# Joining sign, exponent and middle bits in two VectorE steps, in the weight split that opens a convolution and maxout kernel

## The chip, the cores and the metric

The kernel runs on one core of a Trainium2 chip. The metric is the device time of one launch in microseconds, the median of several runs. A core has five engines that run at once: TensorE (PE in the profile, with its weight loads as PEld), VectorE (DVE), ScalarE (ACT), GpSimd (POOL) and SyncE (SP, which here only issues DMA). Each executes its own queue strictly in order and waits on semaphores of the others.

## The reference

```
w   = softmax(weight_gen, over the 7 taps)            # weight_gen: 8 x 4160 x 8 heads x 7
out[s, head] = sum_k w[s, head, k] * x[s - 6 + k, head]   # x: 8 x 4160 x 192, zeros ahead of s = 0
t   = out as 33280 tokens x 192
h   = max(t @ w1, t @ w2, t @ w3)                     # w1, w2, w3: 192 x 768
y   = h @ w_out                                       # w_out: 768 x 192
```

The matrices w1, w2, w3 and w_out arrive as float64. A 64-bit word is read here as two 32-bit words: the high one holds the sign, 11 bits of exponent and the top 20 bits of the mantissa.

## The kernel before

The tokens are cut into 65 chunks of 512 (four columns t of 128 tokens). For each chunk: GpSimd multiplies x with the softmax weights (`product`, L246, tile r; tokens x0.0 to x0.3 in the list below are the four of chunk 0), VectorE sums the seven taps (`total`, L261, tokens +0.0 to +0.3), the result is transposed (`transpose`, tokens t; on TensorE for the first three chunks), and `parts` (tokens p) splits it into a high part (xa_hi, by ScalarE) and a low part (xa_lo, xb: by VectorE for the first three chunks, by GpSimd later). The softmax runs once for three chunks (tokens s0, s1, ...): VectorE red (L215), GpSimd subtract (L217), ScalarE Exp (L222), VectorE den, add, reciprocal (L224 to L226), GpSimd multiply (L229).

TensorE then runs nine `up` steps (k0 to k8: three pairs of column blocks times w1, w2, w3) of 18 matmuls each with 64 rows, the two halves of the rows side by side; a result is copied to m by ScalarE (L376, for w1) or merged into m by VectorE (L378, for w2 and w3). After w3, ScalarE makes h_hi (L381) and GpSimd h_lo (L385). `down` for chunk c-1 (96 matmuls) stands between k5 and k6 of chunk c, and its result is added by ScalarE and VectorE (L410, L411).

The weights must be ready in two parts, hi and lo, before the steps that use them. There are 18 units: a0 to a8 (128x256 each, upper 128 rows of w1 to w3), b0 to b2 (128x384, lower 64 rows of two blocks), d0 to d5 (128x192, w_out). Each goes through the generator `split` (L453 to L498), which issues its instructions in stages; a `yield` ends a stage. Before, one unit takes on VectorE five instructions: clamp (L481), shift and mask (L483), sign joined (L488), then the low bits (L494) and the exponent (L495) for the low part; on ScalarE four: absolute value (L470), a copy of the 32 middle bits to f (L476), hi (L493), f scaled (L497); on GpSimd the product lo = f * e (L498). All PSUM tiles of the kernel (`ps`, eight banks in turn) are shared by the splits, the transposes and the matmuls.

The order of work in the opening is the hand-written list `OPENING`: for each tick a row of names, and each name issues the next stage of that piece of work (or of what it needs first, through `finish`). A tick is half an `up` step; 22 ticks make a chunk, chunk 0 has no `down`. Tick -1 is all that stands ahead of the first matmul; what is not issued when a step needs it is finished there: `finish(p0)`, `finish(a_k)`, `finish(b_k/3)` ahead of step k of chunk 0, `finish(p1)` ahead of chunk 1 and all d ahead of `down` of chunk 0. From then on fixed places per chunk (`PRODUCTS`, `SUMS`, ...) hold. SP issues the loads at the start in the order super 0 of x, a-weights, b-weights, a-weights, super 1, a-weights, w_out.

Of the kernel before, what the change touches and what calls it, by code (L numbers as in the profile page):

```python
# [17 lines left out]
AF = mybir.ActivationFunctionType
ALU = mybir.AluOpType
AX = mybir.AxisListType  # L20

P = 128

OPENING = {
    -1: (
        "x0.0 x0.1 a0 a0 a1 a0 a1 x0.3 a2 a0 x0.2 a2 +0.0 a2 b0 b0 s1 +0.1 a1 a2 b0 +0.3 s1 "
        "a1 b0 s0 b1 +0.2 s1 a3 a3 a6"  # L30
# [3 lines left out]
    2: "s0",
    3: "a3 x1.0 b1 a6 b2 a5",
    4: "a4 a5 t0",
    5: "a4 x1.1",
    6: "t0",
    7: "s0",
    8: "+1.1 t0 b0 p0 t1 a4 s1 b1",  # L40
    9: "x1.3 a5 a7 b2",
    10: "s0 b2 +1.3",
    11: "+1.2",
    14: "p0 p0 b2",
    16: "a7 a8 p1",
    17: "a7 a8",
    18: "a7 s2 p1 d1",
    19: "d1 t1 a8 p1 b2 d2",
    20: "d2",
    21: "d1 b1 d0",  # L50
    22: "d0",
    24: "t1 +2.0",
    25: "d0 +2.1 d2",
    27: "d5 a8 d1 t1 d0",
    28: "d2 d3 d4",
    29: "d3",
    30: "d4",
    31: "d3 x2.2 d5 d4",
    32: "d5 +2.2 t2 x2.1 t2 x2.3",
    34: "t2 d4 +2.3",  # L60
    35: "x3.0 p2",
    36: "d3",
    37: "x2.0 x3.1 p2 p2",
    40: "+3.0",
    42: "s2",
    43: "t3",
    45: "d5 t3",
    46: "+3.3",
    47: "+3.2",
    49: "x4.1 t3 s2",  # L70
    52: "t3",
    54: "t3",
    55: "p3 x4.0",
    58: "t2",
    63: "+4.1",
    64: "p3",
    66: "s2 t3 x4.2",
    67: "x4.3 +3.1 t3",
    76: "+4.0 x3.3",
    78: "p3",  # L80
    85: "+4.3 +4.2",
    86: "x3.2",
# [8 lines left out]
LOAD = (5, 5)  # L93

ON_TENSOR = 3


@with_exitstack
def lightconv_maxout_kernel(
# [151 lines left out]

    def transpose(c):


        acc = state["acc", c]
        if c < ON_TENSOR:  # L270
            pa, pb = (ps.tile([P, CH], F32, name="ph") for _ in range(2))
            pb = pb[:DB]
            state["p", c] = pa, pb
            for t in range(TC):
                to = slice(t * P, (t + 1) * P)
                pin(nc.tensor.transpose(pa[:, to], acc[:, t, :P], ident))
                pin(nc.tensor.transpose(pb[:, to], acc[:, t, P:], ident))
                yield
            return
        v = xtp.tile([P, NJ * D * 2], F32, name="room", bufs=1)  # L280
        pa, pb = v[:, :CH], v[DB:, CH : 2 * CH]
        state["p", c] = pa, pb
        blocks = v[:, 2 * CH : 2 * CH + TC * D].rearrange("p (t d) -> p t d", t=TC)
        pin(nc.vector.transpose(blocks, acc))  # L284
        yield
        for f in range(0, D, 32):
            to = pa[f : f + 32] if f < P else pb[f - P : f - P + 32]
            to = to.rearrange("f (t p) -> f t p", t=TC)
            for p in range(0, P, 32):
                pin(nc.scalar.copy(to[:, :, p : p + 32], blocks[p : p + 32, :, f : f + 32]))  # L290
            yield

    def parts(c):
# [14 lines left out]
        pin(nc.scalar.copy(xb[:DB], xc[:DB].bitcast(F32)))  # L308
        pin(eng.tensor_tensor(xb[DB:], pb, xc[at].bitcast(F32), op=ALU.subtract))
        state["xT", c] = xa_hi, xa_lo, xb, xc  # L310

# [106 lines left out]
    begun = collections.deque()
    SETTLE = 2.8
# [21 lines left out]
            settle = SETTLE if f is down and args[0] < NC - 1 else 0.0  # L447
            begun.append((clock[0] + settle, f(*args, 1)))


    words = [w.bitcast(U32) for w in (w1, w2, w3, w_out)]

    def split(raw, hi, lo):  # L453

        high = raw[..., 1]


        n = int(np.prod(raw.shape[1:-1]))
        if 2 * n <= CH:
            both = ps.tile([P, CH], F32, name="ph")  # L460
            u, l = both[:, :n], both[:, n : 2 * n]
        else:
            u, l = (ps.tile([P, CH], F32, name="ph")[:, :n] for _ in range(2))
        e, f = (prep.tile([P, NU], F32, name=name, bufs=3)[:, :n] for name in ("e", "f"))
        f_words = f
        if len(raw.shape) == 4:
            u, l, e, f = (v.rearrange("p (i n) -> p i n", n=P) for v in (u, l, e, f))
        ui, li, ei = (v.bitcast(U32) for v in (u, l, e))

        pin(nc.scalar.activation(u, high.bitcast(F32), AF.Abs))  # L470
        yield
# [3 lines left out]
        pin(
            nc.scalar.copy(  # L476
                f_words.bitcast(U16).rearrange("p (n h) -> p n h", h=2),
                flat.bitcast(U16)[..., 1:3],
            )
        )  # L480
        pin(nc.vector.tensor_scalar(u, u, F_MAX, F_MIN, op0=ALU.min, op1=ALU.max))  # L481
        pin(
            nc.vector.tensor_scalar(  # L483
                ui, ui, 3, 0x3FFFF000, op0=ALU.logical_shift_left, op1=ALU.bitwise_and
            )
        )
        pin(
            nc.vector.scalar_tensor_tensor(  # L488
                ui, high, 0xC0000000, ui, op0=ALU.bitwise_and, op1=ALU.bitwise_or
            )  # L490
        )
# [3 lines left out]
        pin(nc.vector.tensor_scalar(ei, ui, 0xFF800000, None, op0=ALU.bitwise_and))  # L495
        yield
        pin(nc.scalar.activation(f, li, AF.Copy, scale=2.0**-36))  # L497
        pin(nc.gpsimd.tensor_tensor(lo, f, e, op=ALU.mult))  # L498
# [206 lines left out]
```

## Time and profile before

| | |
|---|---|
| median of 3 runs | 1698.19 us (1697.55 to 1698.21) |
| the profiled execution | 1699.39 us, span of its instructions 1697.6 us |
| busy over the span | PE 1657.2, PEld 1466.1, DVE 1124.6, ACT 1145.8, POOL 1426.2 us |
| granted TensorE clock, mean | 0.998 |
| HBM traffic | 51.25 MB read, 25.56 MB written, 45 GB/s over the span |

The page lists engines by busy time, the span in 40 slices, the chain of work that ended last, and groups of instructions by line with count, busy time, mean duration and the idle time ahead of them. The group rows name the tile written, then the tiles read, and the shape with partitions first. "Windows" are the same busy times for stretches of the span, "waits" name who was waited for, and the timeline lists instructions in order (neighbours of one kind merged, with their count).

### The profile page before, as it was taken

What the parts mean: (1) busy time and instruction counts of PE and PEld (TensorE: products, weight loads), DVE (VectorE), ACT (ScalarE), POOL (GpSimd) and SP (SyncE); (2) the same over time, 40 slices, a digit from 0 to 9 for tenths busy, and PEclk for the clock granted to TensorE, in tenths of its full rate; (3) what the DMA queues carried; (4) which work ended last, traced back from release to release, by engine and by line L of the source; (5) the groups of instructions that cost most, each with busy time, mean ns of one, the idle gap of its engine ahead of it and who ended that gap; (6) DMA issues with size and microseconds to landing.
All of it is one profiled execution on the core that took longest, in us unless ns stands there. A gap on an engine that the chain in (4) does not pass through costs nothing.

```text
span 1697.6 us, 42191 instructions
## 1 busy us (share of the span) xinstructions
PE 1657.2 (98%) x16794; PEld 1466.1 (86%) x16794; DVE 1124.6 (66%) x1552; ACT 1145.8 (67%) x2896; POOL 1426.2 (84%) x844
## 2 busy tenths in 40 slices
PE   3899999999999999999999999999999999999999
PEld 2598889889889889889988988988988988988998
DVE  7966766666666666666666666666666666666653
ACT  5657667667666766766766766766776776676672
POOL 6888888989888888888888888988888888888872
PEclk9999999999999999999999999999999999999999
DMA  7010101101010110101010110101011010101000
GB/s 236 1 70 10 70 29 52 70 20 60 20 70 15 66 70 21 60 21 70 11 70 21 60 70 20 61 20 70 11 70 61 27 63 20 70 11 46 20 11 29
DMA packets 20422, 79.51 MB, mean 47 GB/s; under 512 B 2320, under 2 KB 5128, under 8 KB 17536
## 3 DMA queue, kind: packets, MB, share of 16 engines
q1 hardware_dynamic: 20104, 76.54, 11.9%
q8 instruction: 131, 2.15, 0.5%
q14 instruction: 67, 0.55, 0.1%
q10 hardware_dynamic: 120, 0.28, 0.0%
HBM read 51.25 MB, written 25.56 MB: 45 GB/s over the span
## 4 chain that ended last, share of the span: by engine, by line
PE 94%; DVE 3%; ACT 1%; DMA 1%; POOL 1%; SPq 0%; issue 0%; DVEq 0%
PE ph L329 94%; DVE acc L261 1%; DVE m L378 0%; DMA wt<-in_weight_gen_dram 0%; DVE ph L483 0%; POOL r L246 0%; DVE ph L488 0%; DVE e L495 0%; DVE ph L481 0%; DVE ph L494 0%; DMA xt<-in_x_dram 0%; SPq L529 0%; ACT room L290 0%; SPq L521 0%; POOL h_lo L385 0%
## 5 line engine op out<-in xcount | busy, mean ns | idle before, releaser
L246 POOL TENSOR_TENSOR r<-xt,wt 128x1344 f32<-128x1344 f32 x260 | 721.4, 2814 | 0.6 <-DMA xt<-in_x_dram 0.4
L378 DVE TENSOR_TENSOR m<-ph,m 128x512 f32<-128x512 f32 x780 | 520.6, 685 | 197.4 <-PE ph L329 113.7
L329 PE MATMUL ph<-xa_hi,wa_hi 64*128 64x512 f32 x2340 | 630.8, 391 | 9.4 <-DVE m L378 3.1
L385 POOL TENSOR_TENSOR h_lo<-m,h_hi 128x512 fp32r<-128x512 f32 x390 | 503.3, 1301 | 161.7 <-ACT h_hi L381 157.0
L329 PE MATMUL ph<-xa_lo,wa_hi 64*128 64x512 f32 x2340 | 626.9, 388 | 1.0 <-DVE xa_lo L304 1.0
L329 PE MATMUL ph<-xa_hi,wa_lo 64*128 64x512 f32 x2340 | 626.1, 387 | 1.1 <-POOL wa_lo L498 1.1
L329 PE MATMUL ph<-xb,wb_hi 64*128 64x512 f32 x2340 | 626.0, 387 | 0.0
L329 PE MATMUL ph<-wo,h_hi 64*128 64x384 f32 x3120 | 595.5, 355 | 0.0
L329 PE MATMUL ph<-wo,h_lo 64*128 64x192 f32 x3120 | 522.3, 247 | 0.0
L381 ACT CAST h_hi<-m 128x512 fp32r<-128x512 f32 x390 | 241.8, 621 | 409.7 <-DVE m L378 406.6
L261 DVE TENSOR_REDUCE acc<-r 128x192 f32<-128x1344 f32 x260 | 401.8, 1547 | 125.5 <-POOL r L246 125.5
L290 ACT COPY room<-room 32x128 f32<-32x128 f32 x1488 | 440.8, 296 | 25.7 <-DVE room L284 7.5
L329 PE MATMUL ph<-xc,wb_lo 64*128 64x512 f32 x1170 | 453.1, 387 | 0.1
L329 PEld LDWEIGHTS ph<-wo,h_lo 64*128 64x128 f32 x3120 | 398.8, 188 | 2.5
L329 PEld LDWEIGHTS ph<-wo,h_hi 64*128 64x128 f32 x3120 | 398.4, 184 | 2.9 <-issue 0.4
L329 PEld LDWEIGHTS ph<-xa_hi,wa_hi 64*128 64x128 f32 x2340 | 338.7, 185 | 53.9 <-DVE m L378 3.9
L329 PEld LDWEIGHTS ph<-xa_hi,wa_lo 64*128 64x128 f32 x2340 | 338.4, 185 | 42.0 <-POOL wa_lo L498 1.5
L329 PEld LDWEIGHTS ph<-xa_lo,wa_hi 64*128 64x128 f32 x2340 | 338.7, 185 | 38.7 <-DVE xa_lo L304 1.5
L329 PEld LDWEIGHTS ph<-xb,wb_hi 64*128 64x128 f32 x2340 | 338.7, 185 | 38.4 <-ACT xb L308 0.3
L376 ACT COPY m<-ph 128x512 f32<-128x512 f32 x390 | 221.8, 586 | 38.5 <-PE ph L329 35.3
L411 DVE TENSOR_TENSOR o<-ph,ob 128x192 f32<-128x192 f32 x260 | 86.7, 353 | 234.5 <-ACT ob L410 234.5
L329 PEld LDWEIGHTS ph<-xc,wb_lo 64*128 64x128 f32 x1170 | 216.3, 185 | 20.9 <-POOL wb_lo L498 0.5
(54 smaller groups left out, 702.6 us busy)
## 6 DMA issues: line engine op xcount, KB each, us to landing
xt<-in_x_dram SPq DMA_DIRECT2D x20, 1728.0 KB, 7.1
out_dram<-o SPq DMA_DIRECT2D x64, 384.0 KB, 2.3
wt<-in_weight_gen_dram SPq DMA_DIRECT2D x21, 336.0 KB, 3.0
h_hi<-in_moe_w_dram SPq DMA_DIRECT2D x6, 256.0 KB, 4.8
xt<-in_x_dram SPq DMA_DIRECT2D x1, 1536.0 KB, 9.3
h_lo<-in_moe_w_dram SPq DMA_DIRECT2D x6, 192.0 KB, 4.8
room<-in_moe_w_out_dram SPq DMA_DIRECT2D x1, 1152.0 KB, 8.1
xt<-in_x_dram SPq DMA_DIRECT2D x1, 960.0 KB, 5.2
```

The source lines that it names most:

```text
L246: nc.gpsimd.tensor_tensor(r.rearrange("p (h g) k -> p k h g", g=G), xt[:, la + t : la + t + K].rearrange("p k (h g) -> p k h g", g=G), wt[ ...
L261: nc.vector.tensor_reduce(state["acc", c][:, t], r, axis=AX.X, op=ALU.add)
L290: pin(nc.scalar.copy(to[:, :, p : p + 32], blocks[p : p + 32, :, f : f + 32]))
L329: ins = nc.tensor.matmul(ph[:, :n], w[h], v[h], start=begins and half == 0 and q == 0, stop=ends and half == 1 and q == len(terms) - 1,)
L376: pin(nc.scalar.copy(m[:, :N], ph[:, :N]))
L378: pin(nc.vector.tensor_tensor(m[:, :N], ph[:, :N], m[:, :N], op=ALU.max))
L381: later(1, lambda: pin(nc.scalar.copy(hi, m[:, :N])))
L385: nc.gpsimd.tensor_tensor(lo, m[:, :N], hi.bitcast(F32), op=ALU.subtract)
L411: pin(nc.vector.tensor_tensor(o[:, t], po[:, :D], ob, op=ALU.add))
```

## The change

Three things change. First, the split. The absolute value u and the middle bits (`low`) are made as before, in one stage. Then the exponent is clamped and shifted to its place by two ScalarE Relus on the upper 16 bits of each word (or, for the nine units in `CLAMP_ON_POOL`, a GpSimd minimum and one Relu); the result goes to the upper halves of `tops`, three tiles that are set to 1 once at the start. VectorE joins in two instructions: `(low >> 13) | tops` to the PSUM tile v, and `(high & sign) | v`. ScalarE makes hi, and lo is now w - hi: on GpSimd for the eight units in `LO_ON_POOL` (for them w is in SBUF), on VectorE from PSUM for the other ten. A unit now has seven stages (a b unit one more, for its four copies to wb_hi). Second, six small GpSimd memsets at the start (`top`, `over`, `span`, `below`). Third, `OPENING` is rewritten. `BY_DMA` is empty, so no copy moves to a DMA queue.

```diff
 OPENING = {
     -1: (
-        "x0.0 x0.1 a0 a0 a1 a0 a1 x0.3 a2 a0 x0.2 a2 +0.0 a2 b0 b0 s1 +0.1 a1 a2 b0 +0.3 s1 "
-        "a1 b0 s0 b1 +0.2 s1 a3 a3 a6"
+        "x0.3 a0 a0 a0 s0 a1 x0.0 a0 a0 a2 x0.1 a1 a0 a1 +0.3 a1 a2 a0 a2 a1 a1 a2 +0.0 b0 a2 "
+        "x0.2 b0 a3 a2 a2 b0 a1 a3 b1 +0.1 b1 +0.2 b0 a3 b0 b1 b0 s1 b0 a3 b1 a3 b0 s1 a4 a5 "
+        "a4 b1 a6 s1 t0 a5 a6 x1.0 a3 a3 x1.2"
     ),
-    0: "a6 a3",
-    1: "a6 b1 a5 t0 +1.0 a4 x1.2",
...
+    1: "a6 a5 a6 a4 a5 b2 a6 b1 a5 p0 a5 s0 a4 x1.1 a7 a6 a4 s1 +1.0 a7 t0 t0",
+    3: "a4 +1.2",
+    8: "b2 a5 b1 b2 a8 x1.3 b2",
+    9: "b2 a7 t0 s0 d1 +1.3 +1.1 b2 a4 a8 t1 b1 a6",
+    16: "a8 a7 b2 b2 a7 a7",
+    17: "d1 x2.2 a8 d1 d0 p0 s2 d0 s0 t1 a7",
...
+    28: "d3",
+    31: "d3 d4",
+    32: "d5 t2 t2 +2.2 d4 d3 d3 x2.1 x2.0",
+    34: "d5",
+    35: "d2 d4 +2.3",
+    36: "p2 t2 x3.0 s2 p2 p2 +3.1",
...
 }
+LO_ON_POOL = ("a2", "a5", "a6", "b0", "d0", "d2", "d3", "d5")
+CLAMP_ON_POOL = ("a4", "a7", "a8", "b2", "d0", "d1", "d2", "d3", "d5")
+BY_DMA = ()
...
+    E_MIN = (1023 - 127) << 4
+    E_MAX = (255 << 4) - 1
     NU = 3 * P
+    top = [const.tile([P, NU], U32, name=f"top{k}") for k in range(3)]
+    turn = itertools.count()
+    over = const.tile([P, 1], F32, name="over")
+    span = const.tile([P, 1], F32, name="span")
+    below = const.tile([P, 1], F32, name="below")
+    F_MAX = float(np.array((E_MIN + E_MAX) << 16 | 0xFFFF, np.uint32).view(np.float32))
...
+    def split(raw, hi, lo, name):
...
+            u, v = both[:, :n], both[:, n : 2 * n]
+            u, v = (ps.tile([P, CH], F32, name="ph")[:, :n] for _ in range(2))
+        if name in CLAMP_ON_POOL:
+            u = prep.tile([P, NU], F32, name="u", bufs=2)[:, :n]
+        tops = top[next(turn) % len(top)][:, :n]
+        low = prep.tile([P, NU], U32, name="low", bufs=3)[:, :n]
         flat = raw.rearrange("p i n w -> p (i n) w") if len(raw.shape) == 4 else raw
+        pin(nc.scalar.activation(u, flat[..., 1].bitcast(F32), AF.Abs))
         pin(
             nc.scalar.copy(
+                low.bitcast(U16).rearrange("p (n h) -> p n h", h=2),
                 flat.bitcast(U16)[..., 1:3],
             )
         )
-        pin(nc.vector.tensor_scalar(u, u, F_MAX, F_MIN, op0=ALU.min, op1=ALU.max))
...
+        yield
+        upper = u.bitcast(U16).rearrange("p (n h) -> p n h", h=2)[..., 1]
+        to = tops.bitcast(U16).rearrange("p (n h) -> p n h", h=2)[..., 1]
+        if name in CLAMP_ON_POOL:
+            pin(nc.gpsimd.tensor_scalar(u, u, F_MAX, None, op0=ALU.min))
+            yield
+            pin(nc.scalar.activation(to, upper, AF.Relu, bias=below, scale=8.0))
+        else:
+            pin(nc.scalar.activation(u, upper, AF.Relu, bias=over, scale=-1.0))
+            yield
+            pin(nc.scalar.activation(to, u, AF.Relu, bias=span, scale=-8.0))
+        yield
+        w = prep.tile([P, NU], F32, name="w", bufs=2)[:, :n] if name in LO_ON_POOL else v
         pin(
             nc.vector.scalar_tensor_tensor(
+                v.bitcast(U32), low, 13, tops, op0=ALU.logical_shift_right, op1=ALU.bitwise_or
             )
         )
         yield
+        pin(
+            nc.vector.scalar_tensor_tensor(
+                w.bitcast(U32),
+                flat[..., 1],
+                0x80000000,
+                v.bitcast(U32),
+                op0=ALU.bitwise_and,
+                op1=ALU.bitwise_or,
+            )
+        )
+        yield
+        if len(raw.shape) == 4:
+            w = w.rearrange("p (i n) -> p i n", n=P)
+        pin(nc.scalar.copy(hi, w))
+        yield
+        eng = nc.gpsimd if name in LO_ON_POOL else nc.vector
+        pin(eng.tensor_tensor(lo, w, hi.bitcast(F32), op=ALU.subtract))
...
+    for t in top:
+        nc.gpsimd.memset(t, 1)
+    nc.gpsimd.memset(over, float(E_MIN + E_MAX))
+    nc.gpsimd.memset(span, float(8 * E_MAX))
+    nc.gpsimd.memset(below, float(-8 * E_MIN))
```

In the prediction, "first join" and "second join" are the two VectorE instructions of the new split; the first reads two tiles in SBUF (`low` and `tops`), the second one in SBUF and one in PSUM.

More of the change, by code (lines that the diff above doesn't have):

```diff
@@ L28 @@
     -1: (
-        "x0.0 x0.1 a0 a0 a1 a0 a1 x0.3 a2 a0 x0.2 a2 +0.0 a2 b0 b0 s1 +0.1 a1 a2 b0 +0.3 s1 "
-        "a1 b0 s0 b1 +0.2 s1 a3 a3 a6"
-    ),
-    0: "a6 a3",
-    1: "a6 b1 a5 t0 +1.0 a4 x1.2",
[L34 to L82, printed above, removed]
[3 rows of a table added]
+    ),
+    1: "a6 a5 a6 a4 a5 b2 a6 b1 a5 p0 a5 s0 a4 x1.1 a7 a6 a4 s1 +1.0 a7 t0 t0",
[4 more added lines that the diff above has]
+    17: "d1 x2.2 a8 d1 d0 p0 s2 d0 s0 t1 a7",
+    18: "d1 d2 p1",
+    19: "d1 t1 a8 p0",
+    20: "d1 d2 d0 d1 d0 d0",
+    21: "p1 d2 d2",
+    24: "d5 d4 a8 d0 t1 +2.0",
+    25: "d5 p1 d4 d3 d2 d5 +2.1",
+    27: "d2 d3 d3 d0 x2.3 s2 d4",
+    28: "d3",
[4 more added lines that the diff above has]
+    36: "p2 t2 x3.0 s2 p2 p2 +3.1",
+    42: "t3",
+    43: "t3 t3 d5 x3.3 x4.1 x4.2 x3.2 +3.2 a8 d5",
+    51: "x4.0",
+    55: "t3 t3 p3 x3.1 +4.1 +4.0 t3 d4 +4.2 x4.3",
+    58: "p3 +3.3",
+    59: "+4.3 +3.0",
+    60: "t2",
+    87: "t3",
+    90: "s2 p3",
 }
@@ L169, in lightconv_maxout_kernel @@
     wo = const.tile([P, NJ, 2 * D], F32R, name="wo")
-    F_MAX = float(np.array(0x47EFFFFF, np.uint32).view(np.float32))
-    F_MIN = float(np.array(0x38000000, np.uint32).view(np.float32))
+    E_MIN = (1023 - 127) << 4
+    E_MAX = (255 << 4) - 1
     NU = 3 * P
+    top = [const.tile([P, NU], U32, name=f"top{k}") for k in range(3)]
[4 more added lines that the diff above has]
+    F_MAX = float(np.array((E_MIN + E_MAX) << 16 | 0xFFFF, np.uint32).view(np.float32))
     halves = (slice(0, DB), slice(DB, P))
@@ L451, in lightconv_maxout_kernel @@
     words = [w.bitcast(U32) for w in (w1, w2, w3, w_out)]
-    def split(raw, hi, lo):
-        high = raw[..., 1]
+    def split(raw, hi, lo, name):
         n = int(np.prod(raw.shape[1:-1]))
@@ L460, in split @@
             both = ps.tile([P, CH], F32, name="ph")
-            u, l = both[:, :n], both[:, n : 2 * n]
+            u, v = both[:, :n], both[:, n : 2 * n]
         else:
[L463 to L471, printed above, removed]
+            u, v = (ps.tile([P, CH], F32, name="ph")[:, :n] for _ in range(2))
[3 more added lines that the diff above has]
+        low = prep.tile([P, NU], U32, name="low", bufs=3)[:, :n]
         flat = raw.rearrange("p i n w -> p (i n) w") if len(raw.shape) == 4 else raw
+        pin(nc.scalar.activation(u, flat[..., 1].bitcast(F32), AF.Abs))
         pin(
             nc.scalar.copy(
-                f_words.bitcast(U16).rearrange("p (n h) -> p n h", h=2),
+                low.bitcast(U16).rearrange("p (n h) -> p n h", h=2),
                 flat.bitcast(U16)[..., 1:3],
@@ L480, in split @@
         )
[L481 to L486, printed above, removed]
+        yield
[11 more added lines that the diff above has]
+        w = prep.tile([P, NU], F32, name="w", bufs=2)[:, :n] if name in LO_ON_POOL else v
         pin(
             nc.vector.scalar_tensor_tensor(
-                ui, high, 0xC0000000, ui, op0=ALU.bitwise_and, op1=ALU.bitwise_or
+                v.bitcast(U32), low, 13, tops, op0=ALU.logical_shift_right, op1=ALU.bitwise_or
             )
@@ L492, in split @@
         yield
-        pin(nc.scalar.copy(hi, u))
-        pin(nc.vector.tensor_scalar(li, f.bitcast(U32), 0x01FFFFFE, None, op0=ALU.bitwise_and))
-        pin(nc.vector.tensor_scalar(ei, ui, 0xFF800000, None, op0=ALU.bitwise_and))
-        yield
-        pin(nc.scalar.activation(f, li, AF.Copy, scale=2.0**-36))
-        pin(nc.gpsimd.tensor_tensor(lo, f, e, op=ALU.mult))
+        pin(
[8 more added lines that the diff above has]
+        )
+        yield
+        if len(raw.shape) == 4:
[4 more added lines that the diff above has]
+        pin(eng.tensor_tensor(lo, w, hi.bitcast(F32), op=ALU.subtract))
     room = [
@@ L544, in prepare_a @@
         pair = slice(2 * jp, 2 * jp + 2)
-        yield from split(raw, wa_hi[:, pair, i], wa_lo[:, pair, i])
+        yield from split(raw, wa_hi[:, pair, i], wa_lo[:, pair, i], f"a{u}")
     def prepare_b(jp):
@@ L549, in prepare_b @@
         hi = prep.tile([P, 3, P], F32R, name="hi", bufs=1)
-        yield from split(raw, hi, wb_lo[:, jp])
+        yield from split(raw, hi, wb_lo[:, jp], f"b{jp}")
+        yield
         for odd, h in enumerate(halves):
             for to in halves:
-                pin(nc.scalar.copy(wb_hi[to, 2 * jp + odd], hi[h].bitcast(F32)))
+                if f"b{jp}" in BY_DMA:
+                    pin(nc.sync.dma_start(out=wb_hi[to, 2 * jp + odd], in_=hi[h]))
+                else:
+                    pin(nc.scalar.copy(wb_hi[to, 2 * jp + odd], hi[h].bitcast(F32)))
     def prepare_down(j):
-        yield from split(raw_down[:, j], wo[:, j, :D], wo[:, j, D:])
+        yield from split(raw_down[:, j], wo[:, j, :D], wo[:, j, D:], f"d{j}")
+    for t in top:
[3 more added lines that the diff above has]
+    nc.gpsimd.memset(below, float(-8 * E_MIN))
     state["now"] = -1
```

## The prediction

> **What bounds the kernel now.** I read the windows first. Columns: stretch in us, its length, busy time and count on PE, PEld, DVE, ACT, POOL, granted clock, DMA share, GB/s.
>
> ```profile
> 9.00:30.00 21.00, 2.71 (x9) 1.21 (x9) 19.19 (x34) 12.59 (x29) 15.50 (x11) 1.00 0.90 284
> 30.00:63.00 33.00, 26.08 (x161) 16.84 (x163) 31.57 (x61) 26.20 (x58) 23.63 (x18) 1.00 0.19 74
> 63.00:82.00 19.00, 16.49 (x120) 11.51 (x118) 18.25 (x36) 9.28 (x25) 18.82 (x15) 0.91 0.00 1
> 95.00:1650.00 1555.00, 1554.80 (x15913) 1384.06 (x15911) 1029.47 (x1379) 1074.29 (x2739) 1339.49 (x779) 1.00 0.12 44
> ```
>
> From 95 us on TensorE is idle for 0.2 us in 1555, so nothing of a change in the opening is lost or won there, as long as GpSimd (86% busy) keeps up: what shifts the opening shifts the end, one for one. In the opening it is VectorE that never rests: 69.0 of the 73 us from 9 to 82. TensorE at its later rate (15913 matmuls in 1555 us, 10.2 per us) would need 28 us for the 290 recorded there. The chain of waits says the same: it runs along VectorE until 77 us, then leaves for TensorE for good, but for one visit to GpSimd.
>
> ```profile
> 76.41 0.37 DVE ph L488
> 77.67 3.90 PE ph L329 x18
> 155.48 5.48 POOL r L246 x2
> 170.18 1523.98 PE ph L329 x14710
> ```
>
> **The change, part by part.** The end of the opening is the first `down` matmul (81.86 us before); I sum what moves it.
>
> *VectorE's instructions.* These are groups of the first 90 us (count, busy us, mean ns, idle ahead). The five groups of a size are equal within 3%; the first and last, or the two of one line, stand for them.
>
> ```profile
> L481 DVE TENSOR_SCALAR ph<-ph 128x256 f32<-128x256 f32 x9 | 3.8, 424 | 2.4 <-ACT ph L470 2.4
> L483 DVE TENSOR_SCALAR ph<-ph 128x256 uint32<-128x256 uint32 x9 | 3.9, 433 | 0.3
> L488 DVE SCALAR_TENSOR_TENSOR ph<-h_hi,ph 128x256 uint32<-128x256 uint32 x6 | 2.6, 429 | 0.2
> L488 DVE SCALAR_TENSOR_TENSOR ph<-room,ph 128x192 uint32<-128x192 uint32 x6 | 2.2, 362 | 0.2
> L488 DVE SCALAR_TENSOR_TENSOR ph<-h_lo,ph 128x384 uint32<-128x384 uint32 x3 | 1.7, 562 | 0.1
> L378 DVE TENSOR_TENSOR m<-ph,m 128x512 f32<-128x512 f32 x20 | 13.3, 683 | 1.7 <-PE ph L329 1.6
> L411 DVE TENSOR_TENSOR o<-ph,ob 128x192 f32<-128x192 f32 x2 | 0.7, 358 | 0.6 <-ACT ob L410 0.6
> ```
>
> Removed: five instructions in each of 18 units, 5 x (9 x 0.427 + 6 x 0.358 + 3 x 0.56) = 38.4 us. Added: two joins per unit at the duration of L488, 2 x (9 x 0.429 + 6 x 0.362 + 3 x 0.562) = 15.4 us; and ten subtractions for lo, of the kind of L411 and L378 (one input in PSUM): on the line between 0.358 us at 192 and 0.683 at 512, 6 x 0.42 + 2 x 0.55 + 2 x 0.36 = 4.3 us. Net 18.7 us less on the engine that was full. Taken alone this would be the gain.
>
> *The first join and GpSimd.* No VectorE instruction of this kernel reads two SBUF tiles; the first join does (`low`, `tops`). One kind shows what a clash with GpSimd looks like, the softmax's add L225, SBUF to SBUF (min/median/max ns; then three of them with what GpSimd ran):
>
> ```profile
> L225 DVE TENSOR_SCALAR den<-den x23: 182/397/827, 6.2 to 1598.9; 128x96 f32<-128x96 f32 x21, 128x32 f32<-128x32 f32 x2
> 26.77 0.21 DVE L225 TENSOR_SCALAR den<-den 128x96 f32<-128x96 f32 x1
> 316.09 0.40 DVE L225 TENSOR_SCALAR den<-den 128x96 f32<-128x96 f32 x1
> 313.59 2.83 POOL L246 TENSOR_TENSOR r<-xt,wt 128x1344 f32<-128x1344 f32 x1
> 1598.87 0.83 DVE L225 TENSOR_SCALAR den<-den 128x32 f32<-128x32 f32 x1
> 1596.87 2.80 POOL L246 TENSOR_TENSOR r<-xt,wt 128x1344 f32<-128x1344 f32 x1
> 1599.73 0.35 DVE L226 RECIPROCAL den<-den 128x32 f32<-128x32 f32 x1
> ```
>
> At 26.77 GpSimd was idle and L225 took 0.21 us. At 316.09 it ended at 316.49, GpSimd's product at 316.42; at 1598.87 it ended at 1599.70, the product at 1599.67, for a tile a third as wide. So L225 is held until the running GpSimd instruction ends. L378, which has one input in PSUM, is not held: 683 ns on average over these 20, in a stretch where GpSimd is mostly busy. The first join lies between: at best it is free like L378, at worst it waits for GpSimd each time. I take the wait, because like L225 it uses SBUF for more than L378 does. By the Trainium skill (SBUF — State Buffer, Who interferes with whom) a VectorE instruction with two SBUF inputs contends with a GpSimd instruction that reads SBUF, and whichever started first makes the other wait to its end. By that rule, the wait that I take holds; L225 agrees with it for its other case, the modes in which VectorE uses two ports, and no run here shows the case of two inputs.
>
> What GpSimd runs in the first 90 us sets how long a wait is:
>
> ```profile
> L246 POOL TENSOR_TENSOR r<-xt,wt 128x1344 f32<-128x1344 f32 x14 | 37.7, 2727 | 0.5 <-DMA xt<-in_x_dram 0.4
> L385 POOL TENSOR_TENSOR h_lo<-m,h_hi 128x512 fp32r<-128x512 f32 x10 | 12.8, 1283 | 1.8 <-ACT h_hi L381 1.8
> L498 POOL TENSOR_TENSOR wa_lo<-f,e 128x256 fp32r<-128x256 f32 x9 | 6.5, 724 | 7.1 <-ACT f L497 7.1
> L498 POOL TENSOR_TENSOR wo<-f,e 128x192 fp32r<-128x192 f32 x6 | 3.4, 593 | 0.2 <-ACT f L497 0.2
> L498 POOL TENSOR_TENSOR wb_lo<-f,e 128x384 fp32r<-128x384 f32 x3 | 3.0, 1009 | 1.4 <-DVE e L495 1.4
> masks.py:199 POOL TENSOR_SCALAR_AFFINE_SELECT ident<-ident 128x128 f32<-128x128 f32 x1 | 0.3, 292 | 0.1
> ```
>
> A join that arrives at a random moment between 7.84 (the first product) and 90 waits (37.7 x 1.36 + 12.8 x 0.64 + 12.9 x 0.36) / 82 = 0.78 us: half of the instruction it meets, times the chance of meeting it. Five joins (a0, a1, a2, a6, a5) stand in the new list among products that run back to back and get 1.36 us; two (b0, a3) come where GpSimd itself waits for s1's red and get none; eleven get 0.78: 6.8 + 8.6 = 15.4 us. VectorE stands still in them, with sums and m copies queued behind, and TensorE behind those. So VectorE's net is -18.7 + 15.4 = -3.3 us. Bounds: 0 and 18 x 2.73 = 49 us of waiting.
>
> *The path to the first matmul.*
>
> ```profile
> 7.84 7.65 POOL L246 TENSOR_TENSOR r<-xt,wt 128x1344 f32<-128x1344 f32 x3 [0.40 <-DMA xt<-in_x_dram]
> 19.03 0.85 DVE L215 TENSOR_REDUCE red<-wt 128x96 f32<-128x672 f32 x1
> 27.84 1.36 POOL L229 TENSOR_TENSOR wt<-wt,den 128x672 f32<-128x672 f32 x1 [3.54 <-DVE den L226]
> 29.96 0.79 PE L329 MATMUL ph<-xa_hi,wa_hi 64*128 64x512 f32 x1 [2.82 <-ACT xa_hi L300]
> 43.86 2.81 POOL L246 TENSOR_TENSOR r<-xt,wt 128x1344 f32<-128x1344 f32 x1
> 48.24 3.00 DVE L261 TENSOR_REDUCE acc<-r 128x192 f32<-128x1344 f32 x2
> ```
>
> VectorE's queue ahead of xa_lo loses 12 instructions of 0.43 on a-units and one of 0.56 (5.7 us) and gains four or five of the waits (3 x 1.36 + 0.78 = 4.9), so TensorE starts no earlier. But s1's red, at 19.03 before, now stands behind three sums of 1.5 us that followed it, and with it the multiply at 27.84 and chunk 1's products: 0 to +4.4 us late. I take half, 2.2, less the cover of 1.6 us between the end of chunk 1's last product (46.67) and its sum (48.24): +0.6.
>
> *ScalarE.* Nine units have two Relus where one scaling of f stood, nine have one for one.
>
> ```profile
> L497 ACT ACTIVATE f<-ph 128x256 f32<-128x256 uint32 x9 | 3.4, 381 | 1.1 <-DVE e L495 0.9
> L470 ACT ACTIVATE ph<-h_hi 128x256 f32<-128x256 f32 x6 | 2.3, 395 | 3.0 <-DMA h_hi<-in_moe_w_dram 3.0
> L476 ACT COPY f<-h_hi 128x512 uint16<-128x512 uint16 x6 | 3.7, 613 | 0.0
> L222 ACT ACT_TABLE_LOAD x1 | 1.3, 1283 | 4.0 <-DVE red L215 4.0
> ```
>
> That is six of 0.38, two of about 0.5 and one of 0.33, 3.6 us on an engine busy 48 of 73 us: hidden. Not hidden is the order: the absolute value and copy of a4, a5 and a6 (3 x 1.01 = 3.0 us) now stand ahead of xa_hi, behind s1's Exp. Bounds 0 and +3.0; ScalarE idles 8.4 us in 9 to 30, so I take +0.7. The operands of Relu are strided 16-bit words as in L476; at worst each costs L476's 0.61 us, 6 us more on ScalarE, within its 25 us of idle time.
>
> *GpSimd.* Ten lo products leave (6 x 0.72 + 2 x 1.01 + 2 x 0.59 = 7.5 us); nine minima come, one input each, at 0.29 (the one-input select that builds `ident`) to the two-input 0.59 to 1.01, say 0.4: 3.6 us. The joins can hold GpSimd in turn, at most 18 x 0.43 = 7.7 us. It idled 14.7 us of the 73 (L498's, L217's and L229's waits): covered. The memsets (three of 384 columns, at most nine times the select's 0.29 for 128, 2.6 us) run at the very start, when GpSimd waits for the first softmax's red and then for x until 7.84. No DMA is added or moved on SP, ScalarE or GpSimd queues.
>
> Sum: -3.3 + 0.6 + 0.7 = -2.0 us. The profiled execution of 1699.39 would be 1697.4; it stands 1.2 us over the median, so I forecast 1696.2 us, -0.12%. A measurement of this kernel tells about 0.2% (3.4 us) from no change; this would be inside it.
>
> **The rivals.**
>
> *The first join does not wait for GpSimd* (as L378). Then VectorE gives -18.7 + 1.3 = -17.4, and GpSimd ends last: the d products of lo ran just ahead of the first `down`.
>
> ```profile
> 79.27 1.69 POOL L498 TENSOR_TENSOR wo<-f,e 128x192 fp32r<-128x192 f32 x3
> 81.86 0.44 PE L329 MATMUL ph<-wo,h_hi 64*128 64x384 f32 x1
> ```
>
> GpSimd's queue up to there loses 7.5 - 3.6 and two products of chunk 3 (5.5) that the new list puts behind: 9.4 us, plus some of the 7.1 us in which it waited for f; I take half, 13 us in all. Time 1685. For it: L378, never held. Against it: L225, and no row with two SBUF inputs that runs free.
>
> *Slower: the joins of a6, a5 and a4 meet x1.0, x1.2 and x1.1 head-on.* Each join frees up as a product starts and waits a whole one: 3 x 2.73 = 8.2 instead of 3.5 us. Behind them on VectorE stand the first m merges; TensorE's k1 wants the PSUM bank that a6 holds; and b2's middle-bit copy wants the `low` tile of a4 (three in turn), with k0's m copies behind it on ScalarE. With s1's chain at 4.4 - 1.6 = 2.8 instead of 0.6, the sum is -2.0 + 4.7 + 2.2 = +4.9: 1703 us. It decides as soon as the first joins wait more than 18.7 / 18 = 1.04 us on average. For it: the order of the list; against it: the waits are then long enough for GpSimd to run dry later.
>
> *Relu needs a table of its own.* One table load served Abs, Copy and Exp; if Relu needs another, s1's and s2's Exp cost four loads of 1.28: +5.1 - 2.0, 1701 us. Little speaks for it.
>
> **How the numbers follow.** Forecast's case (the joins wait, 11 to 19 us in all, and nearly eat the gain): 0.52, own range 1691 to 1700; of it 0.17 faster, 0.31 same, 0.04 slower. No wait: 0.27, faster. Head-on: 0.18, of it 0.16 slower and 0.02 same. Tables: 0.03, slower. Sums: faster 0.44, same 0.33, slower 0.23. The range reaches from below the no-wait case to above the head-on case, 1683 to 1704.
>
> **What would show it.** The groups of the first join: a mean near 0.43 us (256 columns) refutes the wait; 1.1 to 1.4 us, with ends that coincide with ends of GpSimd products, confirms it. VectorE's busy time over the whole run should fall by about 3 us if waits count as busy, by 19 if not. The first matmul should stand at 29 to 33 us, the first `down` at about 80; one near 69 is the first rival, 85 or more the second. A second table load shows the third. Wrong would make me a first matmul well ahead of 28 us, or a GpSimd that holds TensorE after 95 us.

## The result, and the profile after

The changed kernel takes 1738.19 us (median of 6 runs, 1736.75 to 1738.68) beside 1698.53 us for the kernel before (6 runs, 1697.55 to 1699.26). The ratio is 1.0233 with an interval of 1.0219 to 1.0246: 2.3% slower, where 1696.2 was forecast and 1704 was the end of the range. The profiled execution took 1738.25 us, with a span of 1736.4 us.

First the windows of the changed kernel, in the columns and stretches of the prediction:

```profile
9.00:30.00 21.00, 2.67 (x8) 1.17 (x8) 19.07 (x22) 17.39 (x38) 13.78 (x8) 1.00 0.88 261
30.00:63.00 33.00, 26.58 (x153) 17.84 (x155) 29.00 (x40) 25.72 (x58) 27.62 (x19) 0.95 0.23 89
63.00:82.00 19.00, 15.54 (x124) 11.35 (x122) 17.37 (x19) 10.94 (x25) 16.10 (x12) 1.00 0.00 1
95.00:1650.00 1555.00, 1554.57 (x15547) 1359.16 (x15546) 1015.05 (x1352) 1050.15 (x2667) 1329.32 (x765) 1.00 0.12 44
```

The opening looks much as it did before: by 82 us TensorE has recorded 285 matmuls, 290 before. The loss is in the last row. TensorE is idle for only 0.4 us of 1555, the granted clock is 1.00, and yet 15547 matmuls are recorded where there were 15913, 2.3% fewer. An engine that is busy all the time does less. The timeline shows it on one `up` step (18 matmuls). A row gives the start of a pair of matmuls and the stretch that the pair covers; the second row is the same pair one step later. In the kernel before:

```profile
599.63 0.39 PE L329 MATMUL ph<-xa_hi,wa_hi 64*128 64x512 f32 x2
...
601.67 0.39 PE L329 MATMUL ph<-xa_hi,wa_hi 64*128 64x512 f32 x2
```

and in the changed kernel:

```profile
613.72 0.62 PE L289 MATMUL ph<-xa_hi,wa_hi 64*128 64x512 f32 x2
...
615.82 0.62 PE L289 MATMUL ph<-xa_hi,wa_hi 64*128 64x512 f32 x2
```

A step takes 2.04 us before and 2.10 after. The 0.62 is not the length of a matmul: there one half of the rows runs one matmul ahead of the other, which in both kernels happens in a part of every step. The groups of 200 to 1600 us say which instruction grew, with the mean in ns behind the busy time; before, then after:

```profile
L329 PE MATMUL ph<-xa_lo,wa_hi 64*128 64x512 f32 x2002 | 533.7, 386 | 0.0
L329 PEld LDWEIGHTS ph<-xa_hi,wa_hi 64*128 64x128 f32 x2000 | 288.4, 184 | 32.4
```

```profile
L289 PE MATMUL ph<-xa_lo,wa_hi 64*128 64x512 f32 x1959 | 528.4, 392 | 0.0
L289 PEld LDWEIGHTS ph<-xa_hi,wa_hi 64*128 64x128 f32 x1960 | 281.3, 184 | 37.3
```

The matmul grew by 6 ns, the weight load did not. A chunk is read from its first `down` matmul to the next chunk's; first before, then after:

```profile
612.78 0.33 PE L329 MATMUL ph<-wo,h_hi 64*128 64x384 f32 x1
637.97 0.33 PE L329 MATMUL ph<-wo,h_hi 64*128 64x384 f32 x1
```

```profile
600.54 0.34 PE L289 MATMUL ph<-wo,h_hi 64*128 64x384 f32 x1
626.32 0.34 PE L289 MATMUL ph<-wo,h_hi 64*128 64x384 f32 x1
```

It takes 25.19 us before and 25.78 after, the same in every chunk from the fifth `down` on: 0.59 us times 63 later chunks is 37.2 of the 39.7 us lost. From the first `down` to the end of the span the two profiles differ by as much (1615.7 us before, 1653.0 after). The matmuls and their waits are the same in both kernels; what differs in that stretch is where their tiles lie. The new tiles `top`, `over`, `span` and `below` stand in the pool of constants behind the weights. They take 4704 bytes of each partition, and every tile behind that pool (x parts, h parts, m) lies that much further from the weights, which stay where they were.

Now the opening itself. These are the groups of the two joins and of their ScalarE and GpSimd steps in the first 90 us:

```profile
L449 DVE SCALAR_TENSOR_TENSOR ph<-low,top 128x256 uint32<-128x256 uint32 x9 | 14.4, 1606 | 4.5 <-ACT top L445 4.5
L449 DVE SCALAR_TENSOR_TENSOR ph<-low,top 128x192 uint32<-128x192 uint32 x6 | 8.2, 1379 | 1.6 <-ACT top L441 1.6
L449 DVE SCALAR_TENSOR_TENSOR ph<-low,top 128x384 uint32<-128x384 uint32 x3 | 2.8, 942 | 0.0
L455 DVE SCALAR_TENSOR_TENSOR ph<-h_hi,ph 128x256 uint32<-128x256 uint32 x4 | 1.7, 422 | 0.1
L470 DVE TENSOR_TENSOR wa_lo<-ph,wa_hi 128x256 fp32r<-128x256 f32 x6 | 2.5, 416 | 1.4 <-ACT wa_hi L467 1.4
L439 POOL TENSOR_SCALAR u<-u 128x256 f32<-128x256 f32 x3 | 2.7, 903 | 2.1 <-ACT u L427 2.1
L445 ACT ACTIVATE top<-ph,span 128x256 uint16<-128x256 f32 x6 | 3.1, 547 | 0.1
```

The first join (L449) takes 1.61 us on average, the second (L455) 0.42 for the same 256 columns. Below are joins of the first kind: the first of all, and three more with what GpSimd ran beside them:

```profile
10.80 2.48 DVE L449 SCALAR_TENSOR_TENSOR ph<-low,top 128x256 uint32<-128x256 uint32 x1 [4.09 <-ACT top L445]
31.85 7.94 POOL L211 TENSOR_TENSOR r<-xt,wt 128x1344 f32<-128x1344 f32 x3
34.41 5.54 DVE L449 SCALAR_TENSOR_TENSOR ph<-low,top 128x256 uint32<-128x256 uint32 x2 [0.41 <-ACT top L445]
74.03 2.73 POOL L211 TENSOR_TENSOR r<-xt,wt 128x1344 f32<-128x1344 f32 x1
74.09 2.77 DVE L449 SCALAR_TENSOR_TENSOR ph<-low,top 128x192 uint32<-128x192 uint32 x1 [0.94 <-ACT top L441]
```

The join that began at 74.09 ended at 76.86, GpSimd's product at 76.76; the two joins from 34.41 on took about as long as two products, 5.54 us together, and ended at 39.95 behind the third product's 39.79. TensorE's first matmul and first `down`, with the idle time ahead of them in brackets:

```profile
32.26 0.79 PE L289 MATMUL ph<-xa_hi,wa_hi 64*128 64x512 f32 x1 [7.37 <-ACT xa_hi L264]
83.41 0.41 PE L289 MATMUL ph<-wo,h_hi 64*128 64x384 f32 x1 [1.21 <-DVE m L338]
```

They stand 2.3 and 1.5 us later than in the profile of the kernel before.

### The profile page after: what moved, and what is told of

The parts are those of the page before. It is cut to its first block, busy times and chain, and to the rows that moved or that the text cites. A ratio compares the mean times of both kernels' runs of the same rounds, so it can differ in the third digit from the quotient of the medians.

```text
span 1736.4 us, 42158 instructions
## 1 busy us (share of the span) xinstructions
PE 1694.1 (98%) x16794; PEld 1474.7 (85%) x16794; DVE 1132.5 (65%) x1508; ACT 1154.3 (66%) x2905; POOL 1442.8 (83%) x849
## 4 chain that ended last, share of the span: by engine, by line
PE 94%; DVE 3%; POOL 1%; issue 1%; ACT 1%; DMA 0%; DVEq 0%; POOLq 0%; ACTq 0%
PE ph L289 94%; DVE acc L226 1%; DVE ph L449 1%; POOL r L211 0%; POOL u L439 0%; POOL h_lo L345 0%; DVE m L338 0%; DMA xt<-in_x_dram 0%; DVE den L190 0%; DMA h_hi<-in_moe_w_dram 0%; ACT low L429 0%; DVE w L455 0%; ACT wb_hi L528 0%; POOL wa_lo L470 0%; DVE xb L273 0%
## 5 line engine op out<-in xcount | busy, mean ns | idle before, releaser
L211 POOL TENSOR_TENSOR r<-xt,wt 128x1344 f32<-128x1344 f32 x260 | 732.8, 2863 | 0.6 <-DMA xt<-in_x_dram 0.5
L289 PE MATMUL ph<-xb,wb_hi 64*128 64x512 f32 x2340 | 634.7, 394 | 0.3 <-ACT xb L272 0.2
L289 PE MATMUL ph<-xa_hi,wa_lo 64*128 64x512 f32 x2340 | 634.4, 394 | 0.0
L289 PE MATMUL ph<-xa_lo,wa_hi 64*128 64x512 f32 x2340 | 634.1, 393 | 0.0
L289 PE MATMUL ph<-wo,h_hi 64*128 64x384 f32 x3120 | 603.4, 357 | 1.2 <-DVE m L338 1.2
L289 PE MATMUL ph<-wo,h_lo 64*128 64x192 f32 x3120 | 553.3, 247 | 0.0
L289 PE MATMUL ph<-xc,wb_lo 64*128 64x512 f32 x1170 | 458.1, 392 | 2.5 <-DVE wb_lo L470 2.5
L289 PEld LDWEIGHTS ph<-wo,h_lo 64*128 64x128 f32 x3120 | 428.8, 188 | 2.9
L289 PEld LDWEIGHTS ph<-wo,h_hi 64*128 64x128 f32 x3120 | 425.2, 184 | 1.9 <-POOL wo L470 1.6
```

Of the source, the lines that this page charges most:

```text
L211: nc.gpsimd.tensor_tensor(r.rearrange("p (h g) k -> p k h g", g=G), xt[:, la + t : la + t + K].rearrange("p k (h g) -> p k h g", g=G), wt[ ...
L289: ins = nc.tensor.matmul(ph[:, :n], w[h], v[h], start=begins and half == 0 and q == 0, stop=ends and half == 1 and q == len(terms) - 1,)
```

## The experiments

Two theories stood at first: A, that the new addresses of the tiles slow TensorE; B, that the opening leaves the two halves of the rows in another order against each other, and that this order is the slower one. A gap below is a one-tile pool behind the pool named, which moves all that lies behind it.

**1. The changed kernel, tiles back on multiples of 64 bytes.**

```diff
-    below = const.tile([P, 1], F32, name="below")
+    below = const.tile([P, 9], F32, name="below")[:, :1]
```

> The changed kernel with `below` made 64 bytes wide instead of 32, so that every tile behind the constants starts at a multiple of 64 bytes again (they stand at 32 past one in the changed kernel); no instruction differs. Theory A (place: TensorE reads the x tiles more slowly at 32 past a multiple of 64): a step of 18 matmuls goes from 2.10 us back to 2.04, the time to 1698 to 1703 us; the first `down` stays near 83.4, so what is left over 1698.5 is the opening's, about 1.5 us. Theory B (the two row halves of TensorE settle in another pairing, set by the order in which the opening lets them start): 1738 us, step 2.10.

Measured: 1733.63 us (1731.33 to 1735.41), a ratio to the kernel before of 1.0207 (1.0192 to 1.0222), a step 2.09 us. Alignment to 64 bytes alone is not it.

**2. The kernel before, with a gap of 32 bytes behind the constants.**

```diff
+    gap_const = ctx.enter_context(tc.tile_pool(name="gap_const", bufs=1))
...
+    nc.gpsimd.memset(gap_const.tile([P, 1], F32, name="gap_const"), 0.0)
```

> The kernel before with one unused 4-byte tile (32 bytes of room) behind the constants: every tile behind it starts 32 past a multiple of 64. Theory A: step 2.10 us, 1733 to 1738 us. Theory B: 1698.5 us, step 2.04.

Measured: 1734.26 us, 1.0215 (1.0198 to 1.0232), a step 2.10 us. One empty tile in the old kernel, with its old list and old split, costs 36.0 us, nearly what the whole change cost (39.7).

**3. The same with two gaps of 32 bytes, behind the pools `att` and `xtp`,** so that the x parts move by 32, the h parts by 64, and the loaded x and softmax weights not at all.

> The kernel before, only the pool with the x tiles that TensorE streams (xa_hi, xa_lo, xb, xc, and room) at 32 past a multiple of 64, all else at multiples of 64. Theory A with the streamed tiles as the cause: 1730 to 1737 us. If it is the other tiles (h_hi and h_lo as weights of `down`, or GpSimd's xt, wt, r): under 1703. Theory B: 1698.5.

Measured: 1736.03 us, 1.0221 (1.0205 to 1.0236), a step 2.10 us. Moving the x parts and what lies behind them suffices.

**4. Three gaps, behind the constants, `att` and `xtp`:** the tiles between the constants and the x parts move by 32, the x parts by 64, the h parts by 96.

> The reverse: all tiles behind the constants at 32 past a multiple of 64 but the pool of the streamed x tiles. Theory A with the streamed tiles as the cause: 1698 to 1703 us, with GpSimd's products at 2.86 instead of 2.81 us each if its tiles are what slows it. If other tiles are the cause: 1725 to 1738. Theory B: 1698.5.

Measured: 1714.32 us, 1.0094 (1.0079 to 1.0109), a step 2.06 us. With 64 the loss is under half of the others', and it is not zero.

After these four, B is out: a step had one length per kernel, in the first undisturbed chunk as in the last. In the kernel before the halves run together in one part of a step and one matmul apart in another, as in the changed one, and it stays at 2.04. A in its form "multiples of 64" is out too. What fitted was the distance from weights to streamed tiles, with a coarser period. The next three ask for period and reference point.

**5. and 6. The kernel before with a gap of 512 and of 256 bytes behind the constants** (a tile of 128 and of 64 columns in `gap_const`).

> The kernel before, with a gap of 512 bytes (a tile that GpSimd sets once) behind the constants. Theory P: 2.04 us for an up step, 1697.5 to 1699.5 us: a shift alone does no harm when it is 512. If any shift of the streamed tiles from where they lay costs (period above 512): 2.06 to 2.10 us, 1714 to 1736.

> The kernel before, with a gap of 256 bytes in the same place. It sizes the period: 2.04 us and 1698 if the placement counts modulo 256 or less (against it: a distance of 128 gave 2.09), 2.09 to 2.10 and 1733 to 1736 if it counts modulo 512 or more.

Measured: 1698.23 us, ratio 1.0000 (0.9990 to 1.0009), and 1698.61 us, 1.0001 (0.9991 to 1.0010); a step 2.04 us in both. A gap by itself is harmless; the period is 256 bytes or a part of it.

**7. Everything moved by 32 bytes, the weights too.**

```diff
+    ahead = const.tile([P, 1], F32, name="ahead")
     wa_hi = const.tile([P, NJ, 3, P], F32R, name="wa_hi")
```

> The kernel before, with a tile of 4 bytes (padded to 32) ahead of the first weight tile, so that weights and streamed tiles all lie 32 bytes further on, at the same distance from each other. If the distance between streamed tiles and weights counts: 2.04 us, 1698 us. If the addresses themselves count (all of them are multiples of 64 in the kernel before, 32 past one here): 2.10 us, 1734 to 1736 us.

Measured: 1698.40 us, 1.0002 (0.9993 to 1.0012), a step 2.04 us. None of the weights and streamed tiles lies on a multiple of 64 any more, and nothing is lost: the distance counts, not the address. Experiment 2 has everything behind the weights at the same addresses as this one; of the tiles in use, only the weights lie elsewhere.

**8. The changed kernel, with all tiles behind the constants 19 times 256 bytes from their place in the kernel before.** (A shift of 20 times 256 left no room in SBUF for the last pool, 17.84 of 18 kB, so there is no time for it.)

```diff
-    below = const.tile([P, 1], F32, name="below")
+    below = const.tile([P, 48], F32, name="below")[:, :1]
```

> The changed kernel with the tile `below` 192 bytes wide instead of 4, so that the streamed tiles lie 4864 bytes (19 times 256) further from the weights than in the kernel before; computation and order unchanged. Theory P (the distance of streamed tiles and weights modulo 256 sets TensorE's rate): up step 2.04 us, chunk 25.2 us, and only the opening's +1.5 us is left: 1698 to 1702 us. Rival Q (something else in the changed kernel slows TensorE): 2.09 to 2.10 us, 1733 to 1738 us.

Measured: 1701.03 us (11 runs, 1699.02 to 1702.54), 1.0015 (1.0006 to 1.0024), a step 2.04 us, a chunk 25.19. 160 more bytes, unused, take back 37 of the 40 us. Its windows and its first `down`:

```profile
95.00:1650.00 1555.00, 1554.38 (x15906) 1381.43 (x15904) 1031.05 (x1381) 1074.90 (x2740) 1341.05 (x779) 1.00 0.12 44
```

```profile
83.55 0.41 PE L289 MATMUL ph<-wo,h_hi 64*128 64x384 f32 x1 [1.23 <-DVE m L338]
```

The later rate is that of the kernel before again (15906 matmuls beside 15913), and the opening is that of the changed kernel (83.55 beside 83.41). So this kernel shows what the change itself costs: 2.7 us between the medians.

That is no fixed price, for the opening differs from execution to execution. The eleven runs of experiment 8 spread over 3.5 us. In the profile of experiment 1, its fastest run, the same list got its first two joins through in 0.43 us each, shortly before a GpSimd product ended, where the changed kernel's took 2.48 and 0.87; its first `down` stood at 80.59. In the profiles of the kernel before and of experiments 2 to 7 it stood between 80.3 and 82.5.

**9. and 10. The kernel before with gaps of 128 and 64 bytes behind the constants.**

> The kernel before with a gap of 128 bytes behind the constants. Theory P says that it does what the changed kernel did at that distance (first experiment: 2.09 us, 25.7 us a chunk): 1731 to 1734 us. Rival: the slow step there came from the changed kernel itself, and 128 is as good as 256: 2.04 us, 1698 us.

> The kernel before with a gap of 64 bytes behind the constants, x and h tiles alike. Theory P with the step of the fourth experiment, where the x tiles lay 64 off and the h tiles 96: an up step of 2.06 us and 1712 to 1716 us, a down pair of 0.284 to 0.287 us. If 64 is as bad as 128 when all tiles are 64 off: 2.09 us, 1731 to 1734 us. If the h tiles' place does nothing: the fourth experiment's 1714 to within 2 us.

Measured: 1729.82 us, 1.0181 (1.0167 to 1.0195), a step 2.09 us; and 1713.96 us, 1.0089 (1.0075 to 1.0102), a step 2.06 us. Both steps are as the distance says (the first time is 1.2 us below the range named). The h parts moved by 64 in experiment 10 and by 96 in experiment 4, with the same 2.06 us for an `up` step. The table has the kernels so far by the x parts' distance, as the shift against the kernel before, modulo 256. By its tile sizes, weights and x parts of the kernel before lie whole multiples of 256 bytes apart, so the shift is the distance itself modulo 256.

| shift mod 256 | kernels | `up` step, us | time, us |
|---|---|---|---|
| 0 | before; before + 256; before + 512; all moved 32; changed + 160 more | 2.04 | 1698.2 to 1698.6; changed 1701.0 |
| 64 | before, experiments 4 and 10 | 2.06 | 1714.3, 1714.0 |
| 128 | before, experiment 9; changed, experiment 1 | 2.09 | 1729.8; 1733.6 |
| 32, 96 | before, experiments 2 and 3; changed | 2.10 | 1734.3, 1736.0; 1738.2 |

**11. The changed kernel without the second SBUF input.** The last Relu writes a whole word over u in PSUM. The `top` tiles are gone, and with them the single bit that they held below the middle bits; the shift is 256.

```diff
+        tops = u.bitcast(U32)
         if name in CLAMP_ON_POOL:
             u = prep.tile([P, NU], F32, name="u", bufs=2)[:, :n]
-        tops = top[next(turn) % len(top)][:, :n]
...
-            pin(nc.scalar.activation(to, upper, AF.Relu, bias=below, scale=8.0))
+            pin(nc.scalar.activation(tops, upper, AF.Relu, bias=below, scale=8.0 * 65536))
...
-            pin(nc.scalar.activation(to, u, AF.Relu, bias=span, scale=-8.0))
+            pin(nc.scalar.activation(tops, u, AF.Relu, bias=span, scale=-8.0 * 65536))
```

> The changed kernel with the shifted exponent in PSUM: the last Relu writes a whole 32-bit word (scale and bias times 65536) over u's place in PSUM, so the first join reads one SBUF tile and one PSUM tile; the three `top` tiles and their memsets go (with them the single bit that they held below the middle bits), and the streamed tiles lie 256 bytes from their old place. Theory W (the joins wait for GpSimd, 17.7 us in all, and VectorE sets the opening): the first join takes 0.43 us for 256 columns; the first down matmul comes 8 to 17 us earlier than the 83.4 us of the changed kernel, at 66 to 75; 1684 to 1693 us. Rival (another engine or the list holds the opening once VectorE is free): joins at 0.43 us too, but the first down at 80 to 84 us and 1696 to 1701 us. If the joins still take over 1 us, the two SBUF inputs are not what makes them wait.

Measured: 1691.11 us (1690.13 to 1691.39), ratio to the kernel before 0.9953 (0.9939 to 0.9966). It is 7 us faster than the kernel before and 47 us faster than the changed one. Its first joins and its first `down`:

```profile
L446 DVE SCALAR_TENSOR_TENSOR ph<-low,ph 128x256 uint32<-128x256 uint32 x9 | 3.8, 426 | 5.0 <-ACT ph L442 5.0
L446 DVE SCALAR_TENSOR_TENSOR ph<-low,ph 128x192 uint32<-128x192 uint32 x6 | 2.1, 359 | 1.8 <-ACT ph L438 1.8
L446 DVE SCALAR_TENSOR_TENSOR ph<-low,ph 128x384 uint32<-128x384 uint32 x3 | 1.7, 559 | 0.3 <-ACT ph L442 0.2
```

```profile
72.45 0.37 PE L287 MATMUL ph<-wo,h_hi 64*128 64x384 f32 x1
```

With one input in SBUF and one in PSUM the join runs free at 0.43 us, as theory W had it: 7.6 us for the 18, where experiment 8 spends 25.1. Of these 17.5 us, 11.1 arrive at the first `down` (83.55 to 72.45) and 9.9 at the end (1701.03 to 1691.11). Where the other 6 stay, the windows up to each kernel's first `down` show, experiment 8 first:

```profile
9.00:83.55 74.55, 44.51 (x281) 30.19 (x282) 66.54 (x82) 53.66 (x119) 57.99 (x39) 0.98 0.34 112
```

```profile
9.00:72.45 63.45, 40.40 (x281) 28.80 (x283) 49.90 (x83) 52.69 (x120) 55.87 (x39) 1.00 0.40 133
```

VectorE's work falls by 16.6 us, its idle time grows from 8.0 to 13.6 us. GpSimd is now the fullest engine (55.87 of 63.45 us) with ScalarE close behind. The run changes a little more than the operand of the join: the last Relus, which now write to PSUM, take 0.44 us for 256 columns instead of 0.55, and the three `top` tiles that came in turn are gone. The joins' 17.5 us are read directly; what these two add to the 11.1 is not separated.

**12. Only xb, xc and the tiles behind them (the h parts and m) moved by 32 bytes,** in the kernel before.

```diff
+        if c == 0:
+            nc.gpsimd.memset(xtp.tile([P, 1], F32, name="gap", bufs=1), 0.0)
         xb = xtp.tile([P, CH], F32R, name="xb")
```

> The kernel before with a tile of 4 bytes (padded to 32) between xa_lo and xb, so that xa_hi and xa_lo lie where they lay and only xb, xc (and the h tiles behind them) lie 32 bytes off their distance from the weights. If a matmul is stretched by the place of the very tile that it streams: the groups of matmuls that stream xb and xc take 392 to 394 ns, those of xa_hi and xa_lo 386 to 388, an up step 2.04 + 0.06 x 6/18 = 2.06 us, a chunk 25.2 + 9 x 0.02 + 0.12 = 25.5 us, in all 1714 to 1720 us. If something common to all matmuls is slowed (by any tile off its place): all groups alike at 392 to 394 ns, 2.10 us, 1734 to 1736 us. If only the h tiles count, which moved in every slow kernel so far: 386 ns for xa, xb and xc, 2.04 us, about 1706 us.

Measured: 1730.40 us, 1.0183 (1.0165 to 1.0201), a step 2.09 us: none of the three. Below are groups of 200 to 1600 us and a stretch of the timeline:

```profile
L331 PE MATMUL ph<-xa_hi,wa_hi 64*128 64x512 f32 x1968 | 532.0, 394 | 0.0
L331 PE MATMUL ph<-xb,wb_hi 64*128 64x512 f32 x1968 | 529.5, 393 | 0.0
L331 PE MATMUL ph<-xa_hi,wa_lo 64*128 64x512 f32 x1969 | 528.4, 389 | 0.0
L331 PE MATMUL ph<-xa_lo,wa_hi 64*128 64x512 f32 x1967 | 527.3, 390 | 0.0
```

```profile
610.12 0.52 PE L331 MATMUL ph<-xa_hi,wa_hi 64*128 64x512 f32 x2
610.36 0.51 PE L331 MATMUL ph<-xa_lo,wa_hi 64*128 64x512 f32 x2
```

The kernel before has 386 to 388 ns in these rows. Matmuls that stream xa_hi, which had not moved, grew by 6 ns with wa_hi and by 3 with wa_lo; those that stream xb, which had moved, by 7. So a matmul does not pay for its own tile alone. A row of two covers 0.52 us instead of 0.39: the two halves now start about 0.13 us apart, about half of the step from one matmul to the next (0.23). That is not the cost by itself, since experiments 1 and 9 have one step time, 2.09 us, with the halves 30 to 50 ns apart in the one and under 10 in the other. What makes a matmul 6 ns longer stays open: the runs show that the distance decides, and what each distance costs, not which accesses meet.

## Why the prediction was wrong

**The step that failed** is the sentence behind the windows: "From 95 us on TensorE is idle for 0.2 us in 1555, so nothing of a change in the opening is lost or won there, as long as GpSimd (86% busy) keeps up: what shifts the opening shifts the end, one for one." The rows were right, the inference was not: full means that the matmuls' own rate sets the time, and I took that rate as fixed because no instruction of that stretch changes. The change allocates three tiles and three scalars ahead of the streamed tiles. I priced their memsets, not the 4704 bytes. That term is 25.78 - 25.19 = 0.59 us a chunk, 37.2 us in all (experiments 2 and 8), where the sum had zero and no rival named it. "GpSimd that holds TensorE after 95 us" was the only risk I saw there, and it did not come.

**The opening, term by term.** Experiment 8 isolates it: +2.7 us between the medians, where the sum said -2.0. The terms below are read in the changed kernel's own profile, one execution, whose first `down` came 1.5 us later than before.

- *VectorE's instructions.* Counts and durations held: 0.42 us for the second join, 0.35 to 0.55 for the ten lo's.
- *The first join waits for GpSimd*: right, and settled by experiment 11. The waits are 9 x (1.606 - 0.426) + 6 x (1.379 - 0.359) + 3 x (0.942 - 0.559) = 17.9 us by the groups of the changed kernel and of experiment 11, where I had 15.4. Over the whole run VectorE's busy time did not fall by the 3 us that I named as a sign; it rose by 2.2 (1126.8 us in experiment 8, 1124.6 before). The Trainium skill (SBUF — State Buffer, Who interferes with whom) has the rule for two SBUF inputs; no run before showed that case, and now the trace agrees with it: 1.61 us against 0.43.
- *VectorE's net.* In the windows from 9 us to each kernel's first `down` it was busy 66.9 us instead of 68.9, a fall of 2.0 for my 3.3. Of this, 1.6 us is a sum of taps that the new list puts behind the first `down` (11 sums in the window instead of 12), and what is left is near the -18.7 + 17.9 = -0.8 of the terms. Its idle time rose from 4.0 to 7.6 us, which the sum did not have. Waits for ScalarE make 6.4 of the 7.6: first joins wait 3.8 us for the Relus (6.1 in the group rows, but 2.3 of that lies ahead of 9 us, in the wait that ends at 10.80), low-part subtractions 2.2 for hi, and xb 0.4 for xc. Before, such waits made 1.2 of the 4.0; the rest, small gaps between instructions, shrank with their number. Half of the units now pass ScalarE four times before VectorE may touch them (absolute value, middle bits, two Relus), the others three times and GpSimd once; before, VectorE could start after the absolute value. I counted Relus as work on an engine with room and called them hidden, and not as links of the chain.
- *Relu and minimum.* 0.39 to 0.58 us for 192 and 256 columns, where I took 0.33 to 0.38 and bounded by 0.61. GpSimd's minima took 0.73 to 1.17 us instead of 0.4: 7.5 us in all, not 3.6.
- *The path to the first matmul.* +2.3 us, where the sum had +0.7 for ScalarE, with a bound of +3.0. The last transpose of chunk 0 ended earlier than before (24.89 us, 27.14 before), but xa_hi, which follows it on ScalarE, began only at 31.61 (29.32 before), behind s1's Exp and the absolute values and copies of a4, a5 and a6 (27.46 to 30.72). The first matmul still fell into the interval named (29 to 33 us).
- *s1's chain.* Its multiply came 2.6 us later (30.41, 27.84 before) for my 2.2, and the sums behind chunk 1's last product 0.8 later (49.08, 48.24 before) for my +0.6. This term was right.

**The rivals.** No wait: refuted by the groups; as a price it was 1685 us, and experiment 11, which takes the waits away, gives 1691.1. Its reason held (GpSimd is then the fullest engine), but its queue lost less than I credited; the minima, at twice the estimate, account for 3.9 us of that. Head-on joins: those of a6 and a5 did last about a product each (2.77 us), that of a4 found GpSimd idle (0.43 us at 40.64), and the mean wait of all 18, 0.99 us, lies just under the 1.04 where I let it decide. With 1701.0 against its 1703 its number is nearer than the forecast's, but in part by luck: the joins waited 2.5 us more than in the sum, not 4.7, and VectorE's waits for ScalarE, which it does not name, did the rest. No table was loaded for Relu: there is one load in the run, as before.

## What to carry to other kernels

When an engine is full, its time per instruction is the time of the kernel, and an edit can change it without touching that engine: after any change of allocations compare the mean duration of the dominant instruction with before, and if it moved, pad the new tiles (here to a multiple of 256 bytes) before judging the edit. Of a VectorE instruction ask how many inputs lie in SBUF while GpSimd works; moving one of two to PSUM took it from 1.6 to 0.43 us here. An instruction on an engine with room is free only if the bottleneck's next instruction is not waiting for it: here VectorE's waits for ScalarE grew by about 5 us in the opening. And a difference of 1 to 3 us in an opening is read from medians of several runs, not from one profile.

## What the runs showed of the hardware that was not expected

The duration of a 64-row matmul of 512 columns depends on where the streamed tile lies relative to the weights: 386 to 388 ns where that distance was the old one modulo 256 bytes, 387 to 389 at 64 more, 390 to 393 at 32, 96 or 128 more, with the weight loads of these matmuls at 184 to 185 ns in all. The Trainium skill (SBUF — State Buffer, Who interferes with whom) gives TensorE two independent read ports in SBUF, one for the streamed operand and one for the weights, and says that it waits for no other engine; by that, one would not expect the distance to matter, and the measurement decides that it does.
